# An attention block and a mixer on one core: the channel mix in chunks of 512 tokens, and int64 weights decoded another way

## The chip, the core and the metric

The kernel runs on one core of a Trainium2 chip. Five engines matter here: PE (TensorE, the matrix engine), DVE (VectorE), ACT (ScalarE), POOL (GpSimd) and SP (SyncE, which issues every transfer). The time is device microseconds from start to end of one launch.

## The reference

The inputs are `q`, `k`, `v` of 4 batches, 8 heads, 768 positions and 64 columns, and four weight matrices in float64. Every position attends to the first 8 positions and to the 96 positions that end with itself, with a bias that falls with distance; the result is laid side by side to `x` of 768 tokens by 512 columns for each batch. Then comes the mixer:

```python
h  = np.maximum(xt @ w_tok1, 0.0) @ w_tok2      # token mix: over the 768 tokens, through 256
u  = x + h.transpose(0, 2, 1)
h2 = np.maximum(u @ w_ch1, 0.0) @ w_ch2         # channel mix: over the 512 columns, through 1536
return (u + h2).astype(np.float32)
```

The token mix of a batch needs all of that batch's `x`. The channel mix treats every token for itself, so its tokens may be cut anywhere.

## The kernel before

**Precision.** Each factor of a product is split into a high and a low part of fp32r, and three of the four products are added in PSUM. So one block of weights times one block of tokens is three matmuls: `(0,0), (0,1), (1,0)` in the code.

**Attention.** The work is cut into 48 pairs `v` (two heads, 256 positions), 12 for each batch. A pair is: `load` (SP), `q` (scaling, mostly POOL), `S` (scores on PE into two PSUM banks `sp`), `max` (DVE), `exp` (ACT), `sum` and `inv`, `norm` (POOL), transposition of the probabilities (on PE through `tp` and `back` for the first 20 pairs, later by `split` on DVE, a transposing transfer `turn` and `join` on DVE or ACT), `V` (PE, into bank `op`) and `put` (ACT, from `op` into `x`). `S` uses PE by rows, `V` by columns, all else uses the whole array.

**Token mix of batch b.** `N` transposes `x` (`xtp`), `nh`/`nl` split it (`ph` on ACT, `pl` on DVE), `J` multiplies by `W1` (`pj`, 512 columns wide), `jh`/`jl` split again, `U` multiplies by `W2` (`pu`), `ua` adds `x`, `uh` and `ul` split the sum into `u`.

**Channel mix.** Before the change it runs in 8 chunks of 384 tokens, two for each batch, with 12 steps `f` each (`k` numbers the 96 steps). Step k is `F` (12 matmuls into bank `hp`), `fh` (ACT, the high part `hh`), `fl` (DVE, the low part `hl`), and `G` (12 matmuls into four banks `acc`, one for each block of 128 output columns). After the last step `out` adds `u` to `acc` in two DVE instructions (`o<-acc,uh`, then `o<-o,ul`), and `store` writes. The last chunk alone has `u` summed ahead by POOL (`base`).

**Weights.** The float64 weights come as int64 in 30 pieces of 128 by 512: 3 for `W1`, 3 for `W2`, and 24 for the channel mix, where step f of every chunk needs pieces 6+2f (for `F`) and 7+2f (for `G`). A piece is loaded (`w`), and its two 32-bit words are turned into one fp32 number. `down` (ACT) scales the upper word, read as fp32, into the tile `t`; `shift` (DVE) shifts it left by 3; `upper` (DVE) sets the sign from the upper word; `lower` (DVE) sets the last 3 bits from the lower word. Then `high` (ACT, `wc<-t`) and `low` (DVE or POOL, `wc<-t,wc`) split it. Both words are read at a step of 8 bytes. Three tiles `t` are there; one is held from `down` to `low`. All 24 pieces are kept, so the decode is done once, in the first part of the program, while batches 0 and 1 attend.

**What sets the order.** Every operation is added to a `Plan` with an engine (or a choice of engines), a cost, what it follows, a rank, and the tiles and PSUM banks that it takes and gives. `Plan.record` runs through this list in its own clock, gives each free engine the ready operation of lowest rank, and writes the program in that order; `InOrder` then holds each engine to it. So ranks and costs decide nothing on the chip, they only fix the order of each engine's instructions and the PSUM bank of each operation; on the chip an engine waits at the head of its own list. All of these instructions carry one line in the profile, that of the `InOrder` helper (L204 before, L224 after), so the profile is read by the names of tiles: `hp` and `acc` for the channel mix, `pj` and `pu` for the token mix, `sp`, `tp` and `op` for attention, `t`, `w` and `wc` for the decode. A matmul on plain fp32 (`sp`, `op`) leaves two records.

## Time and profile before

| | |
|---|---|
| median of 3 runs | 627.72 us (626.89 to 628.09) |
| profiled execution, span | 625.9 us |
| PE busy | 606.1 us, 97% |
| DVE busy | 353.1 us, 56% |
| ACT busy | 263.7 us, 42% |
| POOL busy | 201.5 us, 32% |
| first instruction of the token mix of batch 1 on PE | 185.30 us |

The span of the profiled execution is 1.8 us under the median of the runs; sums below are made on its scale. Busy time of PE is the union of records that overlap, since a matmul starts while the one ahead of it still drains. So the distance from start to start is what a matmul costs in a row of them, and not the duration in its record.

### The profile page before, as it was taken

What the parts mean: (1) busy time and instruction counts of PE and PEld (TensorE: products, weight loads), DVE (VectorE), ACT (ScalarE), POOL (GpSimd) and SP (SyncE); (2) the same over time, 40 slices, a digit from 0 to 9 for tenths busy, and PEclk for the clock granted to TensorE, in tenths of its full rate; (3) what the DMA queues carried; (4) which work ended last, traced back from release to release, by engine and by line L of the source; (5) the groups of instructions that cost most, each with busy time, mean ns of one, the idle gap of its engine ahead of it and who ended that gap; (6) DMA issues with size and microseconds to landing.
All of it is one profiled execution on the core that took longest, in us unless ns stands there. A gap on an engine that the chain in (4) does not pass through costs nothing.

```text
span 625.9 us, 10528 instructions
## 1 busy us (share of the span) xinstructions
PE 606.1 (97%) x3776; PEld 552.4 (88%) x3776; DVE 353.1 (56%) x922; ACT 263.7 (42%) x718; POOL 201.5 (32%) x307
## 2 busy tenths in 40 slices
PE   6999997999999999999999999999999999999996
PEld 3667886898988999888888999898998999999996
DVE  6999999897842315866753417666842415113112
ACT  6998755663622102565732214466722202111110
POOL 4689755663500201543420204344310204000000
PEclk9999997999999999999999999999999999999999
DMA  7970375241550001378571002676720001001001
GB/s 277 406 258 2 135 251 220 77 153 35 142 118 2 1 0 51 64 178 196 149 143 65 0 1 64 115 148 164 173 48 1 0 1 51 1 0 52 1 0 57
DMA packets 71228, 59.49 MB, mean 95 GB/s; under 512 B 56960, under 2 KB 61184, under 8 KB 71168
## 3 DMA queue, kind: packets, MB, share of 16 engines
q1 hardware_dynamic: 71168, 58.74, 33.4%
q8 instruction: 32, 0.52, 0.4%
q14 instruction: 28, 0.23, 0.1%
HBM read 38.80 MB, written 6.29 MB: 72 GB/s over the span
## 4 chain that ended last, share of the span: by engine, by line
PE 79%; DVE 10%; DMA 3%; issue 3%; POOL 2%; ACT 2%; SPq 0%; POOLq 0%; ACTq 0%; DVEq 0%
PE acc L204 29%; PE hp L204 29%; PE sp L204 5%; PE op L204 5%; DVE t L204 5%; PE pj L204 4%; PE pu L204 4%; DMA e<-pk 3%; DVE pp L204 2%; PE xtp L204 1%; ACT p L204 1%; PE tp L204 1%; POOL pp L204 1%; DMA p<-r 1%; DVE st L204 0%
## 5 line engine op out<-in xcount | busy, mean ns | idle before, releaser
L204 PE MATMUL hp<-uh,wc 128*128 128x384 f32 x768 | 211.5, 338 | 1.6 <-POOL wc L204 1.5
L204 PE MATMUL acc<-hh,wc 128*128 128x384 f32 x768 | 199.4, 340 | 0.0
L204 DVE SCALAR_TENSOR_TENSOR hl<-hp,hh 128x384 fp32r<-128x384 f32 x96 | 53.1, 553 | 167.3 <-ACT hh L204 167.3
L204 PEld LDWEIGHTS hp<-uh,wc 128*128 128x128 f32 x768 | 140.5, 189 | 5.6 <-POOL wc L204 2.2
L204 PEld LDWEIGHTS acc<-hh,wc 128*128 128x128 f32 x768 | 137.4, 188 | 7.4 <-issue 5.8
L204 ACT ACTIVATE hh<-hp 128x384 fp32r<-128x384 f32 x96 | 46.9, 489 | 220.4 <-PE hp L204 203.8
L204 PE MATMUL acc<-hl,wc 128*128 128x384 f32 x384 | 129.0, 336 | 0.0
L204 PE MATMUL hp<-ul,wc 128*128 128x384 f32 x384 | 128.8, 335 | 0.0
L204 POOL TENSOR_SCALAR p<-p,st 128x256 f32<-128x256 f32 (+1 forms) x132 | 77.4, 604 | 51.9 <-DVE st L204 27.3
L204 DVE COPY r<-p 128x1024 uint16<-128x1024 uint16 (+1 forms) x90 | 64.2, 728 | 35.6 <-DMA p<-r 17.2
L204 POOL TENSOR_TENSOR ul<-x,uh 128x384 fp32r<-128x384 f32 x25 | 26.5, 1060 | 174.2 <-ACT uh L204 99.9
L204 PEld LDWEIGHTS acc<-hl,wc 128*128 128x128 f32 x384 | 72.4, 188 | 0.1
L204 PEld LDWEIGHTS hp<-ul,wc 128*128 128x128 f32 x384 | 72.4, 189 | 0.0
L204 ACT ACTIVATE p<-p,st 128x256 f32<-128x256 f32 (+1 forms) x132 | 63.6, 485 | 20.1 <-DVE st L204 14.9
L204 DVE SCALAR_TENSOR_TENSOR t<-w,t 128x512 int32<-128x512 int32 x60 | 57.1, 952 | 1.2
L204 PE MATMUL sp<-e,qs 64*128 64x256 f32 (+1 forms) x320 | 43.1, 399 | 9.3 <-DVE qs L204 4.0
L204 PEld LDWEIGHTS sp<-e,qs 64*128 64x128 f32 x320 | 28.6, 202 | 17.9 <-DVE qs L204 4.0
L204 POOL TENSOR_SCALAR qs<-e,sc 128x256 f32<-128x256 f32 x37 | 23.5, 636 | 62.8 <-issue 22.1
L204 POOL TENSOR_TENSOR wc<-t,wc 128x512 fp32r<-128x512 f32 x19 | 28.0, 1473 | 18.5 <-ACT wc L204 16.7
L204 POOL TENSOR_SCALAR pp<-pp,st 128x256 f32<-128x256 f32 (+1 forms) x54 | 30.5, 580 | 10.3 <-DVE st L204 7.4
L204 ACT COPY r<-p 128x1024 uint16<-128x1024 uint16 (+1 forms) x22 | 28.5, 1310 | 10.0 <-DMA p<-r 7.2
L204 ACT COPY x<-op 128x256 f32<-128x256 f32 (+1 forms) x64 | 18.6, 323 | 26.9 <-PE op L204 26.8
(91 smaller groups left out, 738.6 us busy)
## 6 DMA issues: line engine op xcount, KB each, us to landing
w<-wc SPq DMA_DIRECT2D x24, 512.0 KB, 6.8
e<-pk SPq DMA_DIRECT2D x24, 512.0 KB, 4.1
out<-o SPq DMA_DIRECT2D x32, 192.0 KB, 1.9
e<-pk SPq DMA_DIRECT2D x15, 384.0 KB, 4.1
unit<-pk SPq DMA_DIRECT2D x8, 512.0 KB, 9.5
w<-w SPq DMA_DIRECT2D x6, 512.0 KB, 8.3
p<-r SPq DMA_TRANSPOSE x56, 3.2
e<-pk SPq DMA_DIRECT2D x1, 256.0 KB, 2.6
```

The costliest lines, as they stand in the source:

```text
L204: ins = getattr(self.engine, name)(*args, **kw)
```

## The change

1. **Chunks.** The channel mix runs in 6 chunks `q` of 512 tokens (`W`). Chunks 1 and 4 straddle two batches: 256 tokens of one and 256 of the next. `parts(q)` lists the pieces of a chunk, `spans(b)` the cuts of a batch. There are 72 steps in place of 96, and every matmul of `F` and `G` is 512 columns wide. `U` of a batch is cut where the chunks are, into four of 512 and four of 256 columns in place of eight of 384.
2. **Output.** In all chunks POOL sums `u` ahead (`base`), in a tile `t`, and `out` is one DVE instruction. A straddling chunk stores in two parts.
3. **Decode.** ACT makes the last three bits from one byte of the lower word (`bits`: byte over 32, less 31/64, rounded to an integer) into `t`, then `down` writes the scaled upper word into the first half of the raw tile itself, without gaps. DVE does two passes, `shift` (shift by 3, or with `t`) and `sign`. DVE's own `shift` and `lower` passes are gone, ACT has one instruction more for each piece.
4. **Buffers.** `x` of a batch is four tiles of 768 columns, so `put` is one copy for every pair; 4 tiles for a later batch in place of 8 half ones. Four tiles for `hh`/`hl` in place of 6. Four slots for the pairs' inputs in place of 5, and 3 pairs loaded ahead of the branch in place of 4.
5. **Ranks and costs.** New numbers, by which the planner makes another order on all engines.

```diff
-RING = 5
+RING = 4
 FAR = 20
-FIRST = 4
+FIRST = 3
 PER = H // 2 * NU
 PIECES = 6 + 2 * NF
+W = 512
+CHUNKS = B * S // W
...
+def parts(q):
+    found, at = [], q * W
+    while at < q * W + W:
+        b, s = divmod(at, S)
+        w = min(S - s, q * W + W - at)
+        found.append((b, s, w, at - q * W))
+        at += w
+    return found
...
+def spans(b):
+    return [(q, s, w, o) for q in range(CHUNKS) for a, s, w, o in parts(q) if a == b]
...
-        self.xs = pool("xs", 8)
+        self.xs = pool("xs", 4)
         self.us = pool("us", 8)
-        self.hl = pool("hl", 6)
...
-        self.plan = Plan(dict(w=2 * NF, raw=AHEAD, t=3, p=6, mix=4, q=1, x=8, u0=8, u1=8, hl=6), BUSY,
+        self.plan = Plan(dict(w=2 * NF, raw=AHEAD, t=3, p=6, mix=4, q=1, x=4, u0=8, u1=8, hl=4), BUSY,
...
-        def words():
-            wi = g["w"].bitcast(I32).rearrange("p (n two) -> p n two", two=2)
-            return wi[:, :, 0], wi[:, :, 1]
+        def bits():
+            g["t"] = self.io.tile([P, 512], I32, tag="io", name="t32")
+            low = g["w"].bitcast(U8).rearrange("p (n e) -> p n e", e=8)[:, :, 3]
+            act.activation(out=g["t"], in_=low, func=AF.Copy, scale=1 / 32, bias=-31 / 64)
 
         def down():
-            g["t"] = self.io.tile([P, 512], I32, tag="io", name="t32")
-            act.activation(out=f32(g["t"]), in_=f32(words()[1]), func=AF.Copy, scale=DOWN)
+            up = g["w"].bitcast(F32).rearrange("p (n two) -> p n two", two=2)[:, :, 1]
+            g["d"] = g["w"].bitcast(I32)[:, :512]
+            act.activation(out=f32(g["d"]), in_=up, func=AF.Copy, scale=DOWN)
 
         def shift():
-            dve.tensor_scalar(out=g["t"], in0=g["t"], scalar1=3, scalar2=None, op0=ALU.logical_shift_left)
-        def upper():
-            dve.scalar_tensor_tensor(out=g["t"], in0=words()[1], scalar=-0x80000000, in1=g["t"], op0=ALU.bitwise_and,
+            dve.scalar_tensor_tensor(out=g["t"], in0=g["d"], scalar=3, in1=g["t"], op0=ALU.logical_shift_left,
                                      op1=ALU.bitwise_or)
 
-        def lower():
-            dve.scalar_tensor_tensor(out=g["t"], in0=words()[0], scalar=29, in1=g["t"], op0=ALU.logical_shift_right,
+        def sign():
+            dve.scalar_tensor_tensor(out=g["t"], in0=g["d"], scalar=-0x80000000, in1=g["t"], op0=ALU.bitwise_and,
                                      op1=ALU.bitwise_or)
 
...
-        add(f"down{n}", "act", 0.6, down, [f"w{n}"], r, ["t"])
-        add(f"shift{n}", "dve", 0.45, shift, [f"down{n}"], r)
-        add(f"upper{n}", "dve", 0.75, upper, [f"shift{n}"], r)
-        add(f"lower{n}", "dve", 0.85, lower, [f"upper{n}"], r, (), ["w", "raw"])
-        add(f"high{n}", "act", 0.52, high, [f"lower{n}"], r - 20, ["w"] if n >= 6 else [])
-        add(f"low{n}", dict(dve=0.64, pool=1.35), 0, low, [f"high{n}"], r - 20, (), ["t"])
+        add(f"bits{n}", "act", 0.7, bits, [f"w{n}"], r, ["t"])
+        add(f"down{n}", "act", 0.7, down, [f"bits{n}"], r)
+        add(f"shift{n}", "dve", 0.7, shift, [f"down{n}"], r)
+        add(f"sign{n}", "dve", 0.7, sign, [f"shift{n}"], r, (), ["w", "raw"])
+        add(f"high{n}", "act", 0.63, high, [f"sign{n}"], r - 20, ["w"] if n >= 6 else [])
+        add(f"low{n}", dict(dve=0.73, pool=1.48), 0, low, [f"high{n}"], r - 20, (), ["t"])
...
@@ -474,8 +491,7 @@
                                    start=i == 0, stop=i == len(blocks) - 1)
 
         def put():
-            for m, o, c, w in (((0, 0, 0, 256),), ((0, 256, 0, 128), (1, 0, 128, 128)), ((1, 128, 0, 256),))[j]:
-                act.copy(out=self.x[b, n, m][:, o:o + w], in_=g["op"][:, c:c + w])
+            act.copy(out=self.x[b, n][:, 256 * j:256 * j + 256], in_=g["op"][:, :256])
...
+        segs = spans(b)
+        def place(i):
+            m, c = divmod(i, 4)
+            return (c, *segs[m])
...
         def up(i):
-            m, c = divmod(i, 4)
+            c, q, s, w, o = place(i)
             g[i] = pu = self.bank("pu", b, i)
             n = 0
             for j in range(2):
-                for p, w in ((0, 0), (0, 1), (1, 0)):
-                    self.pe.matmul(out=pu[:, :HC], lhsT=hs[j][p][:, P * c:P * c + P],
-                                   rhs=self.W2[w][:, S * j + HC * m:S * j + HC * m + HC], start=n == 0, stop=n == 5)
+                for p, z in ((0, 0), (0, 1), (1, 0)):
+                    self.pe.matmul(out=pu[:, :w], lhsT=hs[j][p][:, P * c:P * c + P],
+                                   rhs=self.W2[z][:, S * j + s:S * j + s + w], start=n == 0, stop=n == 5)
                     n += 1
...
-            m, c = divmod(i, 4)
-            self.u[b, m, c] = [self.us.tile([P, HC], F32R, tag=f"u{m}", name=n) for n in ("uh", "ul")]
-            act.copy(out=self.u[b, m, c][0], in_=self.x[b, c, m])
+            c, q, s, w, o = place(i)
+            if o == 0:
+                self.u[q, c] = [self.us.tile([P, W], F32R, tag=f"u{q % 2}", name=n) for n in ("uh", "ul")]
+            act.copy(out=self.u[q, c][0][:, o:o + w], in_=self.x[b, c][:, s:s + w])
...
-        for i in range(8):
-            m = i // 4
+        for i in range(4 * len(segs)):
+            c, q, s, w, o = place(i)
             k = r[NS + i]
-            add(f"U{b}{i}", "pe", 1.04, lambda i=i: up(i),
+            end = i // 4 == len(segs) - 1
+            add(f"U{b}{i}", "pe", 6 * (w / 2400 + 0.013), lambda i=i: up(i),
...
-            add(f"ua{b}{i}", "dve", 0.5, lambda i=i: sum_(i), [f"U{b}{i}"], k - 15, (), [("pu", b, i)])
-            add(f"uh{b}{i}", "act", 0.42, lambda i=i: high_u(i), [f"ua{b}{i}"], k - 15, [f"u{m}"] * 2)
-            add(f"ul{b}{i}", dict(pool=1.03, dve=0.49), 0, lambda en, i=i: low_u(i, en), [f"uh{b}{i}"],
-                k - 15, (), ["x"] if b else ["w"] if m else [])
...
+            add(f"ua{b}{i}", "dve", 0.12 + w / 900, lambda i=i: sum_(i), [f"U{b}{i}"], k - 15, (), [("pu", b, i)])
+            add(f"uh{b}{i}", "act", 0.1 + w / 1150, lambda i=i: high_u(i), [f"ua{b}{i}"], k - 15, [f"u{q % 2}"] * 2 if o == 0 else [])
+            add(f"ul{b}{i}", dict(pool=0.1 + w / 410, dve=0.12 + w / 900), 0, lambda en, i=i: low_u(i, en), [f"uh{b}{i}"],
+                k - 15, (), (["x"] if b else ["w"]) if end else [])
...
         def base(c):
-            g["o", c] = o = self.xs.tile([P, HC], F32, tag="x", name="o")
-            uh, ul = self.u[b, 1, c]
+            uh, ul = self.u[q, c]
+            o = self.xs.tile([P, S], F32, tag="x", name="o")[:, :W] if final else self.io.tile([P, W], F32, tag="io", name="o")
+            g["o", c] = o
             pool.tensor_tensor(out=o, in0=f32(uh), in1=f32(ul), op=ALU.add)
 
-        def total(m, c):
-            acc = g["acc", 2 * b + m, c][:, :HC]
-            if ("o", c) in g:
-                dve.tensor_tensor(out=g["o", c], in0=acc, in1=g["o", c], op=ALU.add)
-                return
-            uh, ul = self.u[b, m, c]
-            p, tag = (self.xs, "x") if m or b == B - 1 else (self.hl, "hl")
-            o = g["o", m, c] = p.tile([P, HC], F32, tag=tag, name="o")
-            dve.tensor_tensor(out=o, in0=acc, in1=f32(uh), op=ALU.add)
-            dve.tensor_tensor(out=o, in0=o, in1=f32(ul), op=ALU.add)
...
+        def total(c):
+            dve.tensor_tensor(out=g["o", c], in0=g["acc", c], in1=g["o", c], op=ALU.add)
+        def store(c, b, s, w, o):
+            self.sp.dma_start(out=self.out[b, P * c:P * c + P, s:s + w], in_=g["o", c][:, o:o + w])
+        tag = f"u{q % 2}"
+        ready = [f"u{x}{b}{4 * m + c}" for b in range(B) for m, cut in enumerate(spans(b)) if cut[0] == q
+                 for x in "hl" for c in range(4)]
+        for f in range(NF):
+            k = q * NF + f
+            r = rank("channel", k)
+            add(f"F{k}", "pe", 2.73, lambda k=k: first(k), ready + [f"low{6 + 2 * f}"] + ([f"F{k - 1}"] if k else []),
+                r - 6, [("hp", k)])
...
+            for i, cs in enumerate(((0,), (1,), (2,), (3,)) if k == last else ((0, 1), (2, 3))):
+                add(f"G{k}{i}", "pe", 0.68 * len(cs), lambda k=k, cs=cs: second(k, cs),
+                    [f"fl{k}", f"low{7 + 2 * f}"] + ([f"G{k}{i - 1}"] if i else [f"G{k - 1}1"] if k else []), r,
...
+        for c in range(4):
+            add(f"base{q}{c}", "pool", 1.35, lambda c=c: base(c), [f"F{k}"], r, ["x" if final else "t"], [tag] * 2)
+            add(f"out{q}{c}", "dve", 0.68, lambda c=c: total(c), [f"G{k}{c if k == last else c // 2}", f"base{q}{c}"], r - 30,
+                [], [("acc", q, c)])
+            pieces = parts(q)
+            for i, cut in enumerate(pieces):
+                add(f"store{q}{c}{i}", "sp", 0.7, lambda c=c, cut=cut: store(c, *cut), [f"out{q}{c}"], r - 30, (),
+                    ["x" if final else "t"] if i == len(pieces) - 1 else [])
...
-            self.channel(b)
+        for q in range(CHUNKS):
+            self.channel(q)
...
-        return 8 + 3 * n if n < 8 else 30 + 4 * n
+        return LOADS[0] + LOADS[1] * n if n < 8 else LOADS[2] + LOADS[3] * n
...
             return 10.0 * v
-        if b == 1:
-            return 120 + 8.5 * i
-        return BATCH * b - 60 + 8.5 * i
+        return PAIRS[b - 1][0] + PAIRS[b - 1][1] * i
     if kind == "mix":
         b, k = at
         if b == 0:
             return -20.0 + k
-        return (220 + 2 * k if b == 1 else BATCH * b + 10 + 3 * k)
+        return MIXES[b - 1] + 2.5 * k
     if kind == "channel":
-        b, k = divmod(at[0], 2 * NF)
-        return 150 + 5.0 * k if b == 0 else BATCH * b + 100 + 5.5 * k
-BATCH = 140.0
+        return CHANNEL[0] + CHANNEL[1] * at[0]
+WEIGHTS = [47.0, 11.3, 60.0, 12.0]
+LOADS = [9.6, 4.2, 32.0, 4.0]
+CHANNEL = [150.0, 6.9]
+PAIRS = [(120, 6.8), (254, 9.5), (376, 5.8)]
+MIXES = [200, 359, 458]
```

What the planner makes of it stands out at three places. The first is ACT while pieces of the channel weights are decoded (`t_` and a number is the decode tile, `w_` the raw piece; `t<-w` is `down` before, and `bits` in the change, where `w<-w` is `down`). Before:

```order
L204 COPY p<-tp 128x512 x2
L204 CAST wc<-t_1539 128x512
L204 CAST wc<-t_1615 128x512
L204 ACTIVATE hh<-hp 128x384
L204 ACTIVATE t_1695<-w_1566 128x512
L204 COPY p<-tp 128x512
L204 ACTIVATE t_1708<-w_1606 128x512
L204 COPY x<-op 128x128 x2
L204 CAST wc<-t_1641 128x512
```

In the change:

```order
L224 COPY p<-tp 128x512 x2
L224 CAST wc<-t_1429 128x512
L224 ACTIVATE t_1501<-w_1388 128x512
L224 COPY p<-tp 128x512
L224 CAST wc<-t_1454 128x512
L224 ACTIVATE w_1388<-w_1388 128x512
L224 ACTIVATE t_1522<-w_1417 128x512
L224 ACTIVATE w_1417<-w_1417 128x512
L224 ACTIVATE t_1533<-w_1431 128x512
```

Three instructions of ACT belong to each piece now, and `back`, `put` and `hh` stand between them.

The second place is DVE in the first steps of the channel mix. Before:

```order
L204 TENSOR_SCALAR t_1202<-t_1202 128x512
L204 SCALAR_TENSOR_TENSOR t_1202<-w_920,t_1202 128x512 x2
L204 TENSOR_SCALAR t_1300<-t_1300 128x512
L204 SCALAR_TENSOR_TENSOR t_1300<-w_1106,t_1300 128x512
L204 SCALAR_TENSOR_TENSOR hl<-hp,hh 128x384
L204 SCALAR_TENSOR_TENSOR t_1300<-w_1106,t_1300 128x512
```

In the change:

```order
L224 SCALAR_TENSOR_TENSOR t_1169<-w_816,t_1169 128x512 x2
L224 SCALAR_TENSOR_TENSOR t_1213<-w_844,t_1213 128x512 x2
L224 SCALAR_TENSOR_TENSOR t_1256<-w_898,t_1256 128x512
L224 SCALAR_TENSOR_TENSOR hl<-hp,hh 128x512
L224 SCALAR_TENSOR_TENSOR t_1256<-w_898,t_1256 128x512
```

Each piece has two DVE instructions in place of three.

The third place is PE in the token mix of batch 3, between the last matmul of `J` and the first of `U`. Before, 12 matmuls of `G` and 12 of `F` stand between the two; these are their first rows:

```order
L204 MATMUL pj<-pl,w1h 128x512
L204 MATMUL acc<-hh,wc 128x384 x2
L204 MATMUL acc<-hl,wc 128x384
L204 MATMUL acc<-hh,wc 128x384 x2
L204 MATMUL acc<-hl,wc 128x384
L204 MATMUL acc<-hh,wc 128x384 x2
L204 MATMUL acc<-hl,wc 128x384
L204 MATMUL acc<-hh,wc 128x384 x2
L204 MATMUL acc<-hl,wc 128x384
L204 MATMUL hp<-uh,wc 128x384
```

In the change:

```order
L224 MATMUL pj<-pl,w1h 128x512
L224 MATMUL acc<-hh,wc 128x512 x2
L224 MATMUL acc<-hl,wc 128x512
L224 MATMUL acc<-hh,wc 128x512 x2
L224 MATMUL acc<-hl,wc 128x512
L224 MATMUL pu<-w2h,ph 128x256
```

Six matmuls of the chunk in hand are left there; the next chunk has to wait for this very batch. Counted over the whole order, PE has done 432 matmuls of `F` and `G` (228 and 204, of 2304) when the token mix of batch 1 begins, and 252 (132 and 120, of 1728) in the change. Up to that point the order has, in the kernel before and in the change: on ACT 30 `down` against 30 `bits` and 30 `down`, `put` 32 against 24, `hh` 19 against 11, `back` 22 against 17, `join` 2 against 4, `q` 4 against 2; on DVE 60 decode instructions with two inputs in both, 30 with one input against none, `hl` 19 against 11, `o` 8 against none, `low` 7 against 13, `back` 24 against 27.

More of the change, by code (lines that the diff above doesn't have):

```diff
@@ L462, in values @@
                 g["p"] = g["r"]
-            if b == 0 and j == 0:
-                x = self.wt.tile([P, 1024], F32, tag="w", name="x")
-                self.x[b, n, 0], self.x[b, n, 1] = x[:, :HC], x[:, HC:S]
-            elif b and j < 2:
-                self.x[b, n, j] = self.xs.tile([P, HC], F32, tag="x", name="x")
+            if j == 0:
+                self.x[b, n] = (self.wt.tile([P, 1024], F32, tag="w", name="x")[:, :S] if b == 0 else
+                                self.xs.tile([P, S], F32, tag="x", name="x"))
             g["op"] = op = self.bank("op", v)
@@ L520, in pair @@
         add(f"V{v}", "pe", 0.86 if j else 0.65, values, [f"{late}{v}0", f"{late}{v}1"], r - 10,
-            [("op", v)] + (["w"] if v < H // 2 else ["x"] if b and j < 2 else []), give, "columns")
-        add(f"put{v}", "act", 0.34 if j == 1 else 0.28, put, [f"V{v}"], r - 15, (), [("op", v)])
+            [("op", v)] + (["w"] if v < H // 2 else ["x"] if b and j == 0 else []), give, "columns")
+        add(f"put{v}", "act", 0.3, put, [f"V{v}"], r - 15, (), [("op", v)])
     def tokens(self, b):
@@ L625, in first @@
                 for w, x in ((0, 0), (0, 1), (1, 0)):
-                    self.pe.matmul(out=ps[:, :HC], lhsT=self.A[f][w][:, P * c:P * c + P], rhs=self.u[b, m, c][x],
+                    self.pe.matmul(out=ps, lhsT=self.A[f][w][:, P * c:P * c + P], rhs=self.u[q, c][x],
                                    start=n == 0, stop=n == 11)
@@ L631, in high @@
         def high(k):
-            hid[k][1:] = [self.hl.tile([P, HC], F32R, tag="hl", name=n) for n in ("hh", "hl")]
-            act.activation(out=hid[k][1], in_=hid[k][0][:, :HC], func=AF.Relu)
+            hid[k][1:] = [self.hl.tile([P, W], F32R, tag="hl", name=n) for n in ("hh", "hl")]
+            act.activation(out=hid[k][1], in_=hid[k][0], func=AF.Relu)
         def low(k):
             ps, hh, hl = hid[k]
-            dve.scalar_tensor_tensor(out=hl, in0=ps[:, :HC], scalar=0.0, in1=f32(hh), op0=ALU.max, op1=ALU.subtract)
+            dve.scalar_tensor_tensor(out=hl, in0=ps, scalar=0.0, in1=f32(hh), op0=ALU.max, op1=ALU.subtract)
         def second(k, cs):
@@ L642, in second @@
                 if f == 0:
-                    g["acc", k // NF, c] = self.bank("acc", k // NF, c)
+                    g["acc", c] = self.bank("acc", q, c)
                 for i, (w, p) in enumerate(((0, 1), (1, 1), (0, 2))):
-                    self.pe.matmul(out=g["acc", k // NF, c][:, :HC], lhsT=self.Z[f][w][:, P * c:P * c + P], rhs=hid[k][p],
+                    self.pe.matmul(out=g["acc", c], lhsT=self.Z[f][w][:, P * c:P * c + P], rhs=hid[k][p],
                                    start=f == 0 and i == 0, stop=f == NF - 1 and i == 2)
+        final = q == CHUNKS - 1
@@ new lines, in total @@
+        def total(c):
[10 more added lines that the diff above has]
+                r - 6, [("hp", k)])
+            add(f"fh{k}", "act", 0.6, lambda k=k: high(k), [f"F{k}"], r - 30, ["hl", "hl"])
+            add(f"fl{k}", "dve", 0.68, lambda k=k: low(k), [f"fh{k}"], r - 30, (), [("hp", k)])
+            for i, cs in enumerate(((0,), (1,), (2,), (3,)) if k == last else ((0, 1), (2, 3))):
+                add(f"G{k}{i}", "pe", 0.68 * len(cs), lambda k=k, cs=cs: second(k, cs),
+                    [f"fl{k}", f"low{7 + 2 * f}"] + ([f"G{k}{i - 1}"] if i else [f"G{k - 1}1"] if k else []), r,
+                    [("acc", q, c) for c in cs] if f == 0 else [], ["hl", "hl"] if cs[-1] == 3 else [])
```

55 lines of the change are left out of this document (16 added, 39 removed).

## The prediction

> **What bounds the kernel now.** I read the page's shares first, then the table of stages, cut at 70 us and where the token mix of batch 1 begins, then the chain of waits.
>
> ```profile
> PE 606.1 (97%) x3776; PEld 552.4 (88%) x3776; DVE 353.1 (56%) x922; ACT 263.7 (42%) x718; POOL 201.5 (32%) x307
> 0.00:70.00 70.00, 61.11 (x453) 43.99 (x453) 62.20 (x233) 60.47 (x202) 50.03 (x102) 0.98 0.59 221
> 70.00:185.30 115.30, 109.89 (x684) 100.36 (x683) 96.92 (x192) 59.99 (x148) 59.92 (x64) 0.97 0.48 146
> 185.30:625.90 440.60, 435.08 (x2644) 408.01 (x2642) 193.96 (x498) 143.28 (x370) 91.58 (x142) 1.00 0.26 62
> 185.30 1.83 PE xtp L204 x16
> ```
>
> In the stage rows the columns are the length, then busy time of PE, PEld, DVE, ACT and POOL, then PE's granted clock. After 185.3 us PE is busy for 435.1 of 440.6 us at full clock, and the others for less than half. There only PE's own work counts. Up to 185.3 us DVE is busy for 62.2 + 96.9 = 159.1 us (86%) and ACT for 120.5 us (65%; 86% in the first 70 us). There PE's order and the two engines that feed it lie close together. So the change has two prices: what 512-column matmuls save in the whole, and what the new decode does to the first 185 us.
>
> **Step 1, the channel mix in 1728 matmuls of 512 columns.** The price of one is the distance of starts. For 384 columns it is read from a block of 12 in the chain, for 512 from a row of `pj` on PE's timeline (12 starts apart) and from the chain's block of 24, which includes the slower first ones.
>
> ```profile
> 448.79 2.08 PE hp L204 x12
> 450.87 2.08 PE acc L204 x12
> ...
> 188.17 5.49 PE pj L204 x24
> ...
> 190.32 0.39 PE L204 MATMUL pj<-ph,w1l 128*128 128x512 f32 x1
> ...
> 193.04 0.39 PE L204 MATMUL pj<-ph,w1l 128*128 128x512 f32 x1
> ```
>
> 2.08 / 12 gives 173.3 ns, (193.04 - 190.32) / 12 gives 226.7 ns, 5.49 / 24 gives 228.8 ns. The 53.4 ns between the first two are 128 columns at 0.417 ns; so 384 columns take 160 ns and some 13.3 ns are left for each matmul whatever its width. Before: 2304 x 173.3 = 399.3 us. Changed: 1728 x 226.7 = 391.7 us, or 395.4 us by the slower row. The gain is **7.6 us**, at least 3.9. I take 7.6, since `F` and `G` run in long rows.
>
> [...]
>
> `U` has the same columns: 192 x 173.3 = 33.3 us against 96 x 226.7 + 96 x 120 (256 columns on the same line, an estimate) = 33.3 us.
>
> **Step 2, the first stage.** In the order, 432 matmuls of `F` and `G` precede the token mix of batch 1 before (74.9 us), and 252 now (57.1 us). With the same stalls that mix would begin at 185.3 - 17.8 = 167.5 us. Can the decode and the attention of batch 1 be done by then? The prices:
>
> ```profile
> L204 DVE SCALAR_TENSOR_TENSOR t<-w,t 128x512 int32<-128x512 int32 x60 | 57.1, 952 | 1.2
> L204 DVE TENSOR_SCALAR t<-t 128x512 int32<-128x512 int32 x30 | 16.0, 532 | 0.0
> L204 DVE TENSOR_TENSOR wc<-t,wc 128x512 fp32r<-128x512 f32 x5 | 3.6, 723 | 0.3 <-ACT wc L204 0.3
> L204 ACT ACTIVATE t<-w 128x512 f32<-128x512 f32 x30 | 20.3, 686 | 5.9 <-POOL wc L204 5.8
> L204 ACT CAST wc<-t 128x512 fp32r<-128x512 f32 x24 | 14.8, 624 | 14.4 <-DVE t L204 14.4
> L204 ACT COPY r<-p 128x1024 uint16<-128x1024 uint16 x18 | 24.4, 1362 | 9.4 <-DMA p<-r 6.6 <-DVE r L204 2.5 <-issue 0.3
> ...
> 88.25 0.69 DVE L204 SCALAR_TENSOR_TENSOR t<-w,t 128x512 int32<-128x512 int32 x1
> 89.32 1.52 DVE L204 SCALAR_TENSOR_TENSOR t<-w,t 128x512 int32<-128x512 int32 x1
> ...
> 89.00 1.29 POOL L204 TENSOR_TENSOR wc<-t,wc 128x512 fp32r<-128x512 f32 x1 [1.68 <-ACT wc L204]
> ```
>
> *DVE.* The 8-byte step is not what makes `t<-w,t` slow: alone it takes 0.69 us, as an instruction without gaps does (`wc<-t,wc`, 0.72). It takes 1.52 us when it starts while POOL's `wc` subtraction runs, and ends 0.55 us after it. Both new passes have two inputs in SBUF, so I keep 0.95 us (between 0.69 and 1.52) and count no gain for the missing gaps. What goes is one pass of 0.53 us for each piece, 16.0 us. With the counts of the order (8 `o` at 0.63 and 8 `hl` less, 11 `hl` at 0.69; 6 `low` and 3 `back` more) DVE's 159.1 us become about 141 us, 84% of 167.5.
>
> *ACT.* 30 instructions more. No row reads single bytes; the bounds are 0.62 us (`wc<-t`, no gaps) and 1.36 us (`r<-p`, twice as many elements of 2 bytes at a step). I take 0.686, the same tile at the same step of 8 bytes, for `bits` and for `down`: +20.6 us (18.7 to 40.9). Fewer and merged `put`, `hh`, `back` and `q`, less two more `join`, take off about 5 us. ACT's 120.5 us become some 136 us, 81% of 167.5. It has held 86% in the first 70 us of this trace.
>
> [...]
>
> *The stall that is there now.* Around 100 us PE waits for a bank, and then runs at half clock:
>
> ```profile
> 100.00:110.00 10.00, 7.21 (x24) 5.98 (x25) 9.67 (x27) 6.27 (x19) 6.34 (x6) 0.66 0.66 250
> 103.49 2.07 PE L204 MATMUL sp<-e,qs 64*128 64x256 f32 x6 [2.59 <-ACT x L204]
> 107.57 0.52 PE L204 MATMUL hp<-uh,wc 128*128 128x384 f32 x1
> 107.89 0.52 PE L204 MATMUL hp<-ul,wc 128*128 128x384 f32 x1
> 101.90 0.70 ACT L204 ACTIVATE t<-w 128x512 f32<-128x512 f32 x1 [1.33 <-POOL wc L204]
> 102.98 0.45 ACT L204 COPY x<-op 128x128 f32<-128x128 f32 x2
> PE hp L204 <- POOL wc L204: 1.5, 2, 0.9
> PE sp L204 <- DVE hl L204: 1.2, 2, 0.9
> ```
>
> `put` (`x<-op`) stands in ACT's list behind a `down` that waits for POOL to give back a tile `t`; PE waits 2.59 us for it, 0.9 for `hl` just before, then starts every 0.32 us in place of 0.17 (a clock of 0.66 over these 10 us) and loses some 3 us more. With 1.5 us for `wc` some 8 us hang on the decode. Two passes on DVE pass a tile on sooner, a third instruction on ACT and the earlier take of `t` later. Bounds: all 8 gone, or as much again added. I take a gain of **4 us**, half, since DVE was the fuller one (96.9 of 115.3 us against 60.0).
>
> **Step 3, the rest.** *Token mix of batch 3.* Six matmuls (1.36 us) are left between `J` and `U`, where 24 were (4.16 us). Here is what has to fit in:
>
> ```profile
> 486.64 1.28 ACT L204 ACTIVATE ph<-pj 128x512 fp32r<-128x512 f32 x2 [1.59 <-PE pj L204]
> 487.27 1.38 DVE L204 SCALAR_TENSOR_TENSOR pl<-pj,ph 128x512 fp32r<-128x512 f32 x2 [1.63 <-ACT ph L204]
> 486.90 0.39 PE L204 MATMUL pj<-pl,w1h 128*128 128x512 f32 x1
> ```
>
> `pl` ends at 488.65, 1.5 us after the next matmul could start (487.13): a loss of **0.3 us**. *The end.* The last `out` is 512 wide (0.69 for 0.56 us), and its store a third larger (1.9 us for 192 KB): **+0.8 us**. *Changes of PE's use.* The order has 124 in place of 123, at 0.2 us each (a block after `sp` takes 2.28 for 2.08): +0.2.
>
> ```profile
> out<-o SPq DMA_DIRECT2D x32, 192.0 KB, 1.9
> 454.89 1.06 PE sp L204 x8
> 455.96 2.28 PE hp L204 x12
> L204 DVE TENSOR_TENSOR o<-o,ul 128x384 f32<-128x384 f32 x28 | 19.7, 702 | 1.0
> L204 POOL TENSOR_TENSOR o<-uh,ul 128x384 f32<-128x384 f32 x4 | 3.9, 1016 | 1.3 <-DMA out<-o 1.3
> SPq L204 <- PE op L204: 122.2, 24, 23.7
> ```
>
> *At nothing.* `base` puts 20 instructions of about 1.35 us on POOL (1.016 x 4/3) and takes 28 of 0.70 us off DVE. Two `F` of 2.72 us stand ahead of the next chunk's first `G`; without that cover a chunk would pay up to 4 x 1.35 us. `fh` and `fl` (0.60 + 0.69) hide behind the next `F`; two pairs of `hh`/`hl` are enough for that, and bare they would cost 1.3 us a step. Four input slots make SP's loads wait for a `V` one pair nearer; they wait 122 us on `V` now and PE does not wait for them after 185 us. In the order the nearest `S` stands 6 us of PE's work behind the `V` that frees its slot, and a load lands in 4.1 us.
>
> **Sum.** -7.6 - 4 + 0.3 + 0.8 + 0.2 = -10.3 us. On the profiled execution that is 615.6 us, and with the 1.8 us to the median of the runs **617.4 us**.
>
> **Rivals.**
> *A, ACT becomes the bound of the decode and the kernel gets slower.* ACT's list holds `put`, `hh` and `exp` behind `bits`, `down` and `high`, which wait for a tile `t` (5.8 us now) and for DVE (14.4 us now). Of 136 us ACT has 75.5 left after 70 us. The change loses from the point where the mix of batch 1 begins later than 167.5 + 7.6 - 1.3 = 173.8 us, that is where ACT gets under 73% of its time busy. Between 70 and 185.3 us it has 52% now, though without need for more. At 65% the mix begins at 186.2 us: 627.7 + 12.4 = 640 us. Against it speaks the 86% of the first stage.
> *B, the decode stops mattering.* All 8 us of step 2 go, and four more from the first 70 us, where ACT and DVE are both full: 609 us. Against it: ACT has more to do in those 70 us, not less.
> *C, attention of batches 2 and 3 comes late.* With fewer slots and PE banks held by pairs of `F`, a late load or bank costs PE a third of a microsecond a pair (6 us of distance less 4.1 of landing and some 2 of issue and scaling leave nothing): 24 x 0.33 = 8 us, 625 us. For it: the 6 us above. Against it: no such wait now.
> *M, a matmul costs by its columns alone.* Then the 13.3 ns would belong to the columns, step 1 gains nothing, and the rest leaves 625 us. The slope between the two widths speaks against it. [...]
>
> **How the numbers follow.** Forecast (612 to 621.5 us) 0.48; B below 612 us 0.16; C 0.10 and M 0.03 (621.5 to 626.4 us); within 0.2% of before, which is about what a measurement here can tell, 0.07; A above 629 us 0.16. So faster 0.77, same 0.07, slower 0.16. The range is 606 to 630 us: it leaves out the end of B (0.05) and most of A (0.13).
>
> **What would show it.** Right: blocks of 12 `hp` or `acc` at 2.72 us; the first `xtp` of batch 1 between 158 and 168 us; 1.2 to 1.5 us for `t<-w,t` only while POOL's `wc` runs; ACT 75% to 85% busy up to that mix. Wrong: blocks of 2.76 us and over; `bits` over 0.8 us; PE waits on ACT's `put` or `hh` of more than 8 us in sum before that mix; PE waits for `qs` or a load after it.

## The result, and the profile after

The changed kernel takes **611.57 us** (611.29 to 612.72, four runs), the kernel before beside it 627.68 us (626.89 to 628.09, four runs): 16.1 us less, a ratio of 0.9745 (95% interval 0.9731 to 0.9759). The profiled execution has a span of 609.4 us, against 625.9 before. Ratios compare fast runs alone; of the runs below, one of experiment 1 (667.74 us) and one of the second part of experiment 4 (3335.96 us) were slow ones.

The page's shares and the table of stages of the changed kernel, cut at 70 us and at the first transposition of the token mix of batch 1 (columns: length; busy time of PE, PEld, DVE, ACT and POOL; PE's granted clock):

```profile
PE 592.3 (97%) x3200; PEld 468.7 (77%) x3200; DVE 329.9 (54%) x856; ACT 269.8 (44%) x699; POOL 212.4 (35%) x312
...
0.00:70.00 70.00, 61.21 (x461) 45.75 (x462) 59.13 (x225) 61.70 (x198) 46.03 (x102) 1.00 0.59 219
70.00:157.04 87.04, 86.20 (x493) 67.36 (x493) 80.53 (x165) 72.60 (x161) 55.81 (x59) 1.00 0.57 179
100.00:110.00 10.00, 10.00 (x66) 7.98 (x63) 8.34 (x18) 8.34 (x21) 7.60 (x8) 1.00 0.78 262
157.04:609.40 452.36, 444.86 (x2249) 355.55 (x2247) 190.29 (x468) 135.46 (x342) 110.60 (x152) 1.00 0.27 63
```

The mix begins at 157.04 us, where it began at 185.30 (185.13 by PE's timeline, from which 157.04 and the starts below are taken) and 163.5 was forecast (167.5 less 4). PE is busy for 86.2 of the 87 us ahead of it. The ten microseconds from 100 us, in which PE was busy for 7.21 us at a clock of 0.66, are full now at full clock. Up to the mix DVE is busy for 59.13 + 80.53 = 139.7 us (89%), ACT for 134.3 us (86%).

The chain of waits (start, length, what) has blocks of 12 at 2.72 us and of 24 at 5.44, both 226.7 ns a matmul:

```profile
476.29 2.72 PE acc L224 x12
480.37 2.72 PE acc L224 x12
483.09 2.72 PE hp L224 x12
...
489.89 5.44 PE acc L224 x24
495.33 5.44 PE hp L224 x24
```

The costliest groups of the decode and the output (count, busy time, mean ns of one, idle time before it and what ended that):

```profile
L224 DVE SCALAR_TENSOR_TENSOR t<-w,t 128x512 int32<-128x512 int32 x60 | 50.7, 855 | 2.1 <-ACT w L224 1.3
L224 POOL TENSOR_TENSOR o<-uh,ul 128x512 f32<-128x512 f32 x24 | 33.5, 1422 | 90.6 <-DMA out<-o 90.6
L224 ACT ACTIVATE t<-w 128x512 int32<-128x512 uint8 x30 | 20.5, 682 | 1.1 <-POOL wc L224 0.8 <-DVE wc L224 0.4
L224 ACT ACTIVATE w<-w 128x512 f32<-128x512 f32 x30 | 20.4, 679 | 0.3
L224 ACT CAST wc<-t 128x512 fp32r<-128x512 f32 x24 | 14.9, 622 | 11.9 <-DVE t L224 11.7
```

`bits` reads single bytes in 0.682 us, `down` takes 0.679. ACT's wait for POOL to give back a tile `t` is 0.8 us (5.8 before). `t<-w,t` stays far above the 0.69 us that it takes alone. PE's waits, first up to the mix of batch 1, then behind it (us in total, times, longest):

```profile
PE sp L224 <- DVE n L224: 4.2, 1, 4.2
PE sp L224 <- issue: 1.9, 1, 1.9
PE tp L224 <- DVE pp L224: 1.4, 1, 1.4
PE sp L224 <- ACT qs L224: 0.8, 1, 0.8
...
PE acc L224 <- DVE hl L224: 2.0, 3, 1.0
```

The first is the start of the program, which the kernel before has too. None is for `x`, for POOL's `wc`, or for a load.

**Where the 16 us are.** Each matmul record of the two traces is priced by the distance of starts in undisturbed rows (0.4167 ns a column + 13.4 ns for `hp`, `acc`, `pu`, `pj`, fitted to starts 120, 173.4 and 226.7 ns apart at 256, 384 and 512 columns; the same per column + 0.8 ns for each of the two records of plain fp32, the two being mostly 216 ns at 256 columns; 109 ns for a transposition). The rest of PE's time is waits, half clock and changes of PE's use.

| us | before | after | difference | prediction |
|---|---|---|---|---|
| PE's own work, priced so | 567.4 | 559.7 | -7.7 | -7.6 |
| rest, up to the mix of batch 1 | 37.5 | 27.2 | -10.3 | -4 |
| rest, from there to the last matmul | 15.1 | 16.8 | +1.7 | +0.5 |
| from the last matmul's start to the end | 5.8 | 5.7 | -0.1 | +0.8 |
| sum | | | -16.4 | -10.3 |

So the question is the second row. Cut by time, the rest up to the mix falls by 2.5 us in the first 70 us (23.1 to 20.6; the clock there was 0.98 and is 1.00), by 2.2 us from 70 to 100 us (3.4 to 1.2) and by 5.8 us from 100 to 110 us (6.4 to 0.6), and it grows by 0.2 us from there to the mix (4.6 to 4.8). Of the 27.2 us that are left, 20.6 lie in the first 70 us.

### The profile page after: what moved, and what is told of

It is laid out like the page before. It is cut to its first block, busy times and chain, and to the rows that moved or that the text cites. A ratio compares the mean times of both kernels' runs of the same rounds, so it can differ in the third digit from the quotient of the medians.

```text
span 609.4 us, 9214 instructions
## 1 busy us (share of the span) xinstructions
PE 592.3 (97%) x3200; PEld 468.7 (77%) x3200; DVE 329.9 (54%) x856; ACT 269.8 (44%) x699; POOL 212.4 (35%) x312
## 5 line engine op out<-in xcount | busy, mean ns | idle before, releaser
L224 PE MATMUL hp<-uh,wc 128*128 128x512 f32 x576 | 186.5, 392 | 0.3
L224 PE MATMUL acc<-hh,wc 128*128 128x512 f32 x576 | 181.1, 395 | 0.0
L224 ACT ACTIVATE hh<-hp 128x512 fp32r<-128x512 f32 x72 | 42.9, 596 | 194.7 <-PE hp L224 194.6
L224 DVE SCALAR_TENSOR_TENSOR hl<-hp,hh 128x512 fp32r<-128x512 f32 x72 | 49.6, 689 | 145.0 <-ACT hh L224 144.8
L224 PEld LDWEIGHTS hp<-uh,wc 128*128 128x128 f32 x576 | 108.1, 188 | 25.8 <-issue 1.7
L224 PEld LDWEIGHTS acc<-hh,wc 128*128 128x128 f32 x576 | 105.6, 188 | 26.2 <-issue 5.5
L224 PE MATMUL acc<-hl,wc 128*128 128x512 f32 x288 | 112.6, 391 | 2.0 <-DVE hl L224 2.0
L224 PE MATMUL hp<-ul,wc 128*128 128x512 f32 x288 | 112.1, 389 | 0.0
L224 DVE COPY r<-p 128x1024 uint16<-128x1024 uint16 (+1 forms) x92 | 68.0, 750 | 31.2 <-POOL p L224 20.3
L224 POOL TENSOR_TENSOR o<-uh,ul 128x512 f32<-128x512 f32 x24 | 33.5, 1422 | 90.6 <-DMA out<-o 90.6
L224 PE MATMUL op<-r,e 128*64 128x128 f32 (+1 forms) x304 | 29.4, 321 | 0.7 <-DVE r L224 0.7
```

The costliest lines, as they stand in the source:

```text
L224: ins = getattr(self.engine, name)(*args, **kw)
```

## The experiments

The edits of experiments 1, 3 and 4 are given in short, not as they stand in the code; `...` marks what is left out.

**1. The new decode alone, in the order of the kernel before.**

```diff
 down:  (ACT)
-   activation(t, upper word, scale=DOWN)
+   activation(t, byte 3 of the lower word, 1/32, -31/64); activation(d, upper word, scale=DOWN)
 shift, upper:  (DVE)
-   t <<= 3;  t |= upper & sign
+   t |= d << 3;  t |= d & sign
 lower:  (DVE)
-   t |= lower >> 29
+   nothing
```

> The kernel before, in its own order, with the new decode alone (ACT: `bits` and `down` one behind the other in the place of `down`; DVE: `shift` and `upper` become the two new passes, `lower` goes). 384-column matmuls stay. Theory D: the first stage wins what went beyond the forecast, 8 to 11 us, so 617 to 620 us; the wait of ACT for POOL's `wc` (5.8 us) and the half clock at 102 us go. Theory R: 0 to 3 us, 625 to 628 us. If ACT's 20 us more decide (rival A): slower than 630 us.

Measured: 627.39 us, ratio 1.0003 (0.9989 to 1.0018). This is Theory R: neither the gain of Theory D nor the loss of rival A. DVE's work up to the mix falls from 159.1 to 144.2 us, ACT's rises from 120.5 to 139.5 us, and the mix begins at 185.4 us, as it did. The stall stays (the half clock behind it is shorter, 0.83 over the ten microseconds from 100 in place of 0.66). A stage row, a group and three rows of the timeline of that kernel:

```profile
0.00:185.36 185.36, 172.27 (x1132) 145.68 (x1133) 144.18 (x394) 139.49 (x378) 104.55 (x165) 0.97 0.53 174
...
L205 ACT CAST wc<-t 128x512 fp32r<-128x512 f32 x24 | 14.4, 618 | 0.9 <-DVE t L205 0.9
...
98.86 0.69 ACT L205 ACTIVATE t<-w 128x512 int32<-128x512 uint8 x1 [1.33 <-POOL wc L205]
...
104.37 0.41 ACT L205 COPY x<-op 128x128 f32<-128x128 f32 x2
...
104.84 1.15 PE L205 MATMUL sp<-e,qs 64*128 64x256 f32 x6 [2.56 <-ACT x L205]
```

`put` (`x<-op`) still stands in ACT's list behind the pieces of the decode, and PE waits 2.56 us for it (2.59 before). ACT waits 0.9 us for DVE there, where it waited 14.4 us, but its own work has grown by 19 us: `put` comes no sooner. ACT's wait for POOL to give back a tile `t` is still there as well, 5.4 us in all (5.8 before). The new decode together with a fourth tile was not run in this order.

**2. A fourth tile `t` for the kernel before,** in the same order, to take away ACT's wait for POOL.

```diff
-        self.io = pool("io", 3)
+        self.io = pool("io", 4)
```

> The kernel before with a fourth tile `t` in the pool and nothing else: the order of every engine stays, only `down` finds a tile one piece earlier. Theory T (the stall around 102 us is `put` behind `down`s that wait for POOL to give a tile back): ACT's waits on POOL's `wc` (5.8 us) go, PE's 2.59 us for `x` and 0.9 for `hl` go, and with them the half clock behind (some 3 us): 5 to 8 us, 619 to 622 us. Theory S (the decode as a whole is too slow there, a tile more only lets it queue elsewhere): 0 to 2 us, 625 to 628 us.

Measured: 627.35 us, ratio 1.0007 (0.9993 to 1.0020). Two groups on ACT, a stage row, and PE's row:

```profile
L204 ACT ACTIVATE t<-w 128x512 f32<-128x512 f32 x30 | 19.7, 682 | 0.0
L204 ACT CAST wc<-t 128x512 fp32r<-128x512 f32 x24 | 14.8, 622 | 19.5 <-DVE t L204 19.4
...
100.00:110.00 10.00, 7.41 (x25) 6.17 (x26) 9.50 (x26) 6.07 (x19) 6.52 (x7) 0.66 0.67 248
...
103.28 2.07 PE L204 MATMUL sp<-e,qs 64*128 64x256 f32 x6 [2.56 <-ACT x L204]
```

The wait for POOL is gone (5.8 to 0.0 us), and 5.0 us of it come back as a wait for DVE one instruction later (14.4 to 19.4). `put` is as late as it was, and the clock drops as before. Theory S holds.

**3. The new decode with its costs in the plan,** so that an order is made for it; chunks of 384 and the old rank formulas stay.

```diff
-        add(f"down{n}", "act", 0.6, ...), shift 0.45, upper 0.75, lower 0.85, high 0.52, low 0.64 / 1.35
+        add(f"bits{n}", "act", 0.7, ...), down 0.7, shift 0.7, sign 0.7, high 0.63, low 0.73 / 1.48
```

> The kernel before with the new decode and its costs in the plan, so that the order is made for it (chunks of 384 and old rank formulas stay; the token mix of batch 1 stands behind 414 channel matmuls, not 432). In the unchanged order the new decode gave nothing (627.4 against 627.2 us), and its stall at 102 us stayed. Theory O (the order is what wins, the decode only lets it be made): 620 to 626 us, the stall at 102 us moved or gone. Theory S (PE's waits of that stage are set by the pace of tiles `t` and POOL's `wc`, which the new decode does not change): 626 to 629 us.

Measured: 620.21 us, ratio 0.9897 (0.9870 to 0.9924). Theory O holds: the stall is gone, and the mix begins at 175.1 us with 414 channel matmuls ahead of it (by 18 x 173.3 ns = 3.1 us less of them, it would be 182.2 us with the stalls of before):

```profile
100.00:110.00 10.00, 10.00 (x61) 9.68 (x61) 9.45 (x14) 9.06 (x17) 4.95 (x4) 1.00 0.85 313
...
0.00:175.07 175.07, 163.16 (x1115) 138.69 (x1115) 143.45 (x403) 139.88 (x376) 95.97 (x158) 0.99 0.56 183
```

So the decode is worth 0 us in the old order and 7 us in an order made for it. Whether another order could do as much for the old decode at this width was not run; with chunks of 512 it did not (experiment 4).

**4. The old decode in the changed kernel,** first in the places of the new one (`down` for `bits`, `shift` for the first pass, `upper` and `lower` for the second), then with its own costs in the plan.

```diff
 bits:  (ACT)
-   activation(t, byte 3 of the lower word, 1/32, -31/64)
+   activation(t, upper word, scale=DOWN)
 down:  (ACT)
-   activation(d, upper word, scale=DOWN)
 shift, sign:  (DVE)
-   t |= d << 3;  t |= d & sign
+   t <<= 3;  t |= upper & sign;  t |= lower >> 29
```

> The changed kernel with the decode of the kernel before in the places of the new one (ACT: `down` where `bits` was; DVE: `shift` there, `upper` and `lower` in the place of `sign`); every other instruction and its order stays. Theory D (the 6.7 us that came beyond my forecast of the first stage are won by the decode: 16 us less on DVE, tiles `t` free sooner): DVE has 136 + 16 = 152 us to do ahead of the token mix of batch 1; at the 89% of the changed kernel this mix begins at 171 us in place of 157.0, at 97% at 164, and the time is 619 to 625 us. Theory R (the order and the buffers win them): the mix begins at 157 to 159 us, time 611 to 614 us. Theory M (a matmul costs by its columns alone) is out already by the blocks of 12.

> The changed kernel (512-column chunks, new rank numbers, new buffers) with the old decode and the old costs of it in the plan, so that the order is made for it (264 channel matmuls ahead of the token mix of batch 1, not 252). With the old decode in the order made for the new one the time was 625.0 us. Theory P (those 13.4 us are the misfit of the order, the decode itself is worth little): 611 to 616 us. Theory W (DVE's 16 us more of work are the price, whatever the order): 621 to 627 us.

Measured: 624.97 us (ratio 0.9966, 0.9953 to 0.9979) and 625.53 us (0.9982, 0.9966 to 0.9997). The stage rows of the two, up to the mix of batch 1:

```profile
0.00:169.42 169.42, 152.43 (x953) 116.91 (x954) 153.09 (x417) 117.32 (x326) 99.66 (x161) 0.97 0.54 182
```

```profile
0.00:171.60 171.60, 157.36 (x965) 119.19 (x965) 151.57 (x405) 121.06 (x336) 113.93 (x169) 0.97 0.54 182
```

DVE has 153.1 and 151.6 us of work and is 90% and 88% full; the mix begins 12.4 and 14.6 us later (2.7 us of the second are 12 channel matmuls more ahead of it). The first is what Theory D says, the second Theory W: a new plan does not help. With 512-column chunks and the new ranks the old decode costs 13.9 us. DVE has 12 to 13 us more to do there; and the clock of 0.97, where the changed kernel has 1.00, is up to 5 us of the loss (3% of some 170 us, an estimate). In the first of the two it is 1.00 from 100 to 110 us, where PE is full, 0.91 from 110 to 130 us, where PE is busy for 17.4 of the 20 us, and 0.96 from there to the mix (37.3 of 39.4 us).

**5. The old rank formulas,** with the new decode, with the old decode in the new one's places, and with the old decode planned for (the first part of the change alone).

```diff
-        return CHANNEL[0] + CHANNEL[1] * at[0]
+        b, k = divmod(at[0] * 4 / 3, 2 * NF)
+        return 150 + 5.0 * k if b == 0 else 140.0 * b + 100 + 5.5 * k
...   (weights, loads, pairs and mixes: as before the change)
```

> The changed kernel with the rank formulas of the kernel before (those of the channel mix by tokens, k x 96/72). The token mix of batch 1 then stands behind 288 matmuls of the channel mix in place of 252 (8.2 us more). Theory D: the first stage loses no more than the new order would, so that this mix begins at 157.0 + 8.2 = 165.2 us, give or take 2, and the time is 612 to 616 us (up to 4 us for the token mixes of batches 2 and 3, which stand without channel matmuls inside). Theory R: the waits of the kernel before come back, the mix begins at 170 to 174 us, time 618 to 624 us.

> The changed kernel with the old decode and the old rank formulas: chunks of 512, the output by POOL and DVE and the buffers alone. Step 1 of the prediction gives -7.6 us and step 3 +1.3 us; with nothing won in the first stage 621 us (619 to 623). Theory D says this: 619 to 624 us. Theory R too. It tells whether the parts add: new decode and new order together are worth the difference to the changed kernel (611.6 us), and the two single runs above say to which it belongs, or that each alone gives it.

> Chunks of 512, the new output and buffers, with the old decode, its old costs in the plan, and the old rank formulas: the first part of the change alone, in an order made for it (276 channel matmuls ahead of the token mix of batch 1). Steps 1 and 3 of the prediction give 621 us. With the costs of the new decode in the plan it was 645.2 us. Theory P: 624 to 632 us (the old ranks alone cost the changed kernel 20 us, of which the token mixes of batches 2 and 3 have some 6). Theory W: 640 to 646 us.

Measured: 632.09 us (ratio 1.0087, 1.0059 to 1.0116), 645.25 us (1.0286, 1.0264 to 1.0307) and 632.51 us (1.0090, 1.0066 to 1.0115). All are slower than the kernel before, though their matmuls are 7.7 us shorter in sum, and the theories missed them: the first was given at most 624 us, the second too, and the third lies half a microsecond above Theory P's range. My 621 us for the chunks alone was wrong by 11.5 us (by 24 us in the order planned for the other decode). In the account above the planned one has the same rest up to the mix of batch 1 as before (37.7 against 37.5 us) and 27.3 in place of 15.1 us behind it. One place of that is around the token mix of batch 3, which stands bare in these orders. With new decode and old ranks, the chain of waits in the mix, a stage row around it, and PE's waits in those 30 us:

```profile
471.50 6.85 PE pj L224 x30
479.46 1.24 PE pj L224 x3
481.35 1.39 DVE pl L224 x2
482.79 5.29 PE pu L224 x31
...
460.00:490.00 30.00, 25.00 (x138) 19.23 (x137) 15.59 (x26) 9.47 (x17) 6.76 (x9) 1.00 0.28 71
...
PE op L224 <- ACT r L224: 2.2, 1, 2.2
PE op L224 <- DVE r L224: 1.8, 2, 1.1
PE pj L224 <- ACT ph L224: 0.7, 1, 0.7
PE pu L224 <- DVE pl L224: 0.2, 1, 0.2
```

PE is idle for 5 of these 30 us. Most of it (4.0 us) lies ahead of the mix, where `V` of the last pairs of batch 3 (`op`) waits for their transposed probabilities `r`; in the mix `J` waits for `ph`, and `U` for `pl`. No channel matmul stands between. The kernel before has no wait of PE there, and the changed kernel has none of these: their orders cover them. The 4.0 us are late attention, which is what rival C spoke of. The three parts together, each kernel planned for its own decode:

| chunks and ranks | old decode | new decode | worth of the decode |
|---|---|---|---|
| 384, old ranks | 627.2 (before) | 620.2 | 7.0 |
| 512, old ranks | 632.5 | 632.1 | 0.4 |
| 512, new ranks | 625.5 | 611.6 | 13.9 |

These are runs of several sessions; the kernel before beside them moved between 626.96 and 627.68 us, so a difference here is uncertain by some 0.7 us.

**6. ACT's work 20 us up in the changed kernel.**

```diff
             act.activation(out=g["t"], in_=low, func=AF.Copy, scale=1 / 32, bias=-31 / 64)
+            act.activation(out=g["t"], in_=low, func=AF.Copy, scale=1 / 32, bias=-31 / 64)
```

> The changed kernel with `bits` done twice for each piece: 30 x 0.68 = 20.5 us more for ACT, nothing else. Rival A of the prediction said that the decode turns to a loss when ACT becomes its bound. Theory A (ACT, 85% busy up to the token mix of batch 1, is as near to being the bound as DVE): this mix begins at 168 to 178 us in place of 157.0, time 622 to 633 us. Theory N (ACT has room where it counts, DVE alone is the bound): 157 to 161 us, time 611 to 616 us.

Measured: 624.02 us, ratio 0.9958 (0.9939 to 0.9977).

```profile
0.00:167.67 167.67, 151.36 (x952) 113.72 (x953) 141.36 (x389) 151.89 (x388) 101.02 (x163) 0.99 0.55 186
```

ACT has 151.9 us to do, is 91% full, and the mix begins 10.6 us later. 17.6 us more on ACT cost 10.6 us, 13.4 us more on DVE cost 12.4 us (experiment 4). This is Theory A, at the lower end of its times: ACT has no room for that much, and neither has DVE (experiment 4). The changed kernel stands close to where the two meet.

**7. Every `low` of the decode on DVE,** at the same place of the program.

```diff
-            engine.tensor_tensor(out=g["l"], in0=f32(g["t"]), in1=f32(g["h"]), op=ALU.subtract)
+            dve.tensor_tensor(out=g["l"], in0=f32(g["t"]), in1=f32(g["h"]), op=ALU.subtract)
```

> The changed kernel with every `low` of the decode (`wc<-t,wc`) on DVE, at the same place of the program; 14 of them were POOL's. Theory L (a pass of DVE over two SBUF inputs waits while POOL subtracts, and this alone lifts `t<-w,t` from 0.69 to 0.855 us): its mean falls to 0.69 to 0.73 us, 7 to 10 us of DVE's time go, 14 x 0.70 = 10 us come, and DVE stays as full as it was; 607 to 613 us. Theory X (the mean is above 0.69 for another reason): the mean stays over 0.80, DVE has 10 us more to do, 617 to 622 us by the price that 16 us more had with the old decode (13.4 us).

Measured: 614.00 us, 2.4 us more than the changed kernel (ratio to before 0.9799, 0.9775 to 0.9823).

```profile
L224 DVE SCALAR_TENSOR_TENSOR t<-w,t 128x512 int32<-128x512 int32 x60 | 44.8, 756 | 1.8 <-ACT w L224 1.1
...
0.00:158.12 158.12, 147.06 (x953) 112.07 (x954) 141.92 (x406) 135.19 (x358) 78.56 (x145) 1.00 0.58 195
```

Between the two theories: `t<-w,t` falls from 0.855 to 0.756 us, not to 0.69. POOL's `wc` is 60% of the lift. DVE gets 5.9 us off and 9.3 us on, and the mix begins 1.1 us later.

**8. The output by DVE in two instructions, as before.**

```diff
-            pool.tensor_tensor(out=o, in0=f32(uh), in1=f32(ul), op=ALU.add)
...
-            dve.tensor_tensor(out=g["o", c], in0=g["acc", c], in1=g["o", c], op=ALU.add)
+            dve.tensor_tensor(out=g["o", c], in0=g["acc", c], in1=f32(uh), op=ALU.add)
+            dve.tensor_tensor(out=g["o", c], in0=g["o", c], in1=f32(ul), op=ALU.add)
```

> The changed kernel with the output as it was before: DVE adds `uh` and then `ul` to `acc` (two instructions), POOL's 24 `base` go. The prediction costed the new output at nothing for five chunks and took 20 passes of DVE off the late part. Theory Z (DVE and POOL have room there, two `F` of 2.72 us cover the output): the same time up to the last chunk, where the last `out` has one pass more of 0.7 us: 611.5 to 613 us. Theory B (four outputs of two passes, 4 x 1.4 = 5.6 us, hold the banks of `acc` longer than the two `F` last): each of the five chunk changes costs 0.3 to 2 us, 613 to 621 us.

Measured: 614.67 us (ratio 0.9805, 0.9785 to 0.9826); the profiled span is 611.1 us. DVE's last rows with it, and in the changed kernel:

```profile
605.19 0.68 DVE L224 TENSOR_TENSOR o<-acc,uh 128x512 f32<-128x512 f32 x1
605.90 0.69 DVE L224 TENSOR_TENSOR o<-o,ul 128x512 f32<-128x512 f32 x1
```

```profile
602.20 2.73 DVE L224 TENSOR_TENSOR o<-acc,o 128x512 f32<-128x512 f32 x4 [2.15 <-PE acc L224]
```

The time lies in Theory B's range, but the trace shows Theory Z with a longer end. The last matmul starts 1.0 us earlier than in the changed kernel, so the five chunk changes cost nothing, as the prediction said. But the last four outputs run one behind the other: 606.59 in place of 604.93 us. I had counted one pass of 0.7 us there, and four count. The kernel before summed ahead in its last chunk too, so this is no part of the 16 us.

**9. Other numbers for the order,** with nothing else changed.

```diff
-WEIGHTS = [47.0, 11.3, 60.0, 12.0];  LOADS = [9.6, 4.2, 32.0, 4.0];  CHANNEL = [150.0, 6.9]
-PAIRS = [(120, 6.8), (254, 9.5), (376, 5.8)];  MIXES = [200, 359, 458]
+WEIGHTS = [44.7, 15.24, 141.4, 12.93];  LOADS = [9.57, 4.0, 9.77, 5.4];  CHANNEL = [150.6, 6.9]
+PAIRS = [(118.1, 5.65), (241.7, 10.94), (375.9, 5.89)];  MIXES = [192.4, 354.2, 413.8]
...   (SOON [0.061, 0.648], TURN 102.37, costs of down 0.77, sign 0.725, low 0.715)
```

> The changed kernel with other numbers in the order alone: ranks of weights, loads, pairs and token mixes, and two costs (`down` 0.77, `sign` 0.725). 252 channel matmuls stay ahead of the token mix of batch 1, 762 in place of 804 ahead of that of batch 2. Theory R (the order is where the rest is to be won): PE's waits of the first stage fall by 2 to 4 us and those at the token mixes by 1 to 2, the mix of batch 1 begins at 152 to 155 us, time 606 to 609 us. Theory F (the order is at its floor, a matter of luck to a few us): 610 to 615 us.

Measured: **608.08 us** (607.59 to 608.69), ratio to before 0.9697 (0.9679 to 0.9714): 3.5 us under the changed kernel and the fastest of all, a time of Theory R. But the place is another than expected. The mix of batch 1 begins at 156.6 us, 0.5 us earlier. In the account the rest between the mixes of batches 1 and 2 falls from 8.8 to 5.9 us, and PE waits only once behind the first mix:

```profile
PE hp L224 <- ACT x L224: 0.4, 1, 0.4
```

## Why the prediction was right, and where it was not

The time fell by more than forecast: 611.6 us lies in the range (606 to 630), 0.4 us below the lower end of the forecast's own case (612 to 621.5), at the upper end of rival B. That it lies in the range is in part luck: the room below 612 us was left for rival B, whose reason did not come true.

- **Step 1 held.** -7.7 us against -7.6; the blocks are at 2.72 us to the digit. Rival M is out: the 13.3 ns beside the columns are there at both widths, and at 256 columns too (173.4, 226.7 and 120 ns from start to start).
- **The prices of step 2 held.** `bits` and `down` 0.682 and 0.679 us (0.686 taken), no gain from reading without gaps (`t<-w,t` takes 0.684 us on average with POOL idle, 0.69 alone before), one pass of DVE less. DVE's work up to the mix is 139.7 us (141 forecast), ACT's 134.3 (136).
- **The step that failed is "With the same stalls that mix would begin at 167.5 us" with "I take a gain of 4 us, half"**: -4 us, which measured -10.3. I carried the stalls of the old order along as a fixed sum and let the decode cure half of one. Experiments 1 and 2 show that the decode cures none of it in that order, nor does a tile more: `put` stays where it is in ACT's list, and ahead of it one wait gives way to another or to more work. Experiment 3 shows that a new order removes it, and in the changed kernel 8.0 us go between 70 and 110 us (2.2 + 5.8), as much as the upper bound that I had named. The other 2.3 us (2.5 less 0.2) come from the first 70 us, to which I had given nothing. I had both engines' work right and read their share (84% and 81%) as room. With the new ranks (the changed kernel and experiments 4, 6, 7, 8 and 9) the fuller engine of the two is 88% to 91% busy up to the mix, and 141 us of DVE's work over 0.89 would have given 158 us. But this share could not be known ahead: with the old ranks it is 78% to 89%, and in the kernel before 86%. Nor is it shown to be the bound of the changed kernel, where PE itself is busy for 86.20 of the 87.04 us from 70 us on. What experiments 4 and 6 show is that there is little room left: 12 to 18 us more work on either engine delay the mix by 11 to 15 us.
- **Rival A did not come.** ACT did not become the bound at 86%. It does with 17.6 us more (experiment 6), and the upper bound for `bits` and `down` (40.9 us, 20.3 more than taken) would have brought that; but even then the time is 624.0 us, under the kernel before, where the rival gave 640.
- **Rival B's price (-12 us in the first stage) was nearer than the forecast's.** It had 8 us for the stall and 4 for the first 70 us, which measured 8.0 and 2.5. But its reason, a decode that stops mattering, is refuted: 13 us more of it on DVE cost 12.4 us.
- **Step 3.** The tail did not grow (-0.1 and not +0.8): the last `out` ends 1.2 us behind the last matmul's start (1.0 before), but the end follows 4.5 us later (4.8 before). In its place PE waits 2.0 us for `hl`, which I had called hidden behind the next `F`; the rest behind the first mix is +1.7 for +0.5. The 0.3 us at the mix of batch 3 were not there (the rest from that mix to the last matmul's start is under 0.1 us, 0.35 before), and my own figures for it, 1.5 less 1.36 us, come to less than 0.2. `base` at nothing is confirmed up to the last chunk (experiment 8). Of the waits for `qs` or a load that rival C needs, the changed kernel has none behind the first mix.

- **The marks.** The mix at 157.0 us and ACT at 86% lie a little outside those given (158 to 168 us, 75% to 85%), the one early, the other fuller. `t<-w,t` is lifted by more of POOL's work than `wc` alone (below).

What is open: why the new decode gains so little with 512-column chunks and the old ranks. By the medians it is 0.4 us, by the profiled executions 2.5 us (the runs of that kernel spread over 4.2 us): the rest up to the mix is 34.6 us against 37.7 with the old decode, and 0.6 us more behind it. No single wait accounts for it.

## What to carry to other kernels

Where the order of in-order engines is planned, the parts of a change do not add: wider matmuls alone lost 5.5 us, the decode alone was worth between 0 and 13.9 us, and only the order made for both gave 16. For a stage that two engines feed, do not forecast its length as the old length with its stalls less something. Set the fuller engine's work beside it too, over a share that such a stage reaches (here 0.78 to 0.91, by the order), and take both as bounds. Before crediting a freed resource with a stall, look at what stands next in the same engine's list.
